# Two sigmoids behind the next unit's first copy, and a VectorE product behind the doubling, in the last batch of an attention and feed-forward kernel

## The chip, the cores and the metric

The kernel runs on one core of one Trainium2 chip. The metric is the device time of one launch in microseconds, the median of several runs. Five engines work side by side, each through its own queue in order: TensorE (PE) multiplies matrices into PSUM, ScalarE (ACT) applies functions, VectorE (DVE) and GpSimd (POOL) do elementwise work, and SyncE (SP) issues most transfers. An instruction that must wait for another engine holds all that stands behind it on its own queue.

## The reference

The first half is clustered attention: each query and key is assigned to the nearest of 16 centroids by cosine, and a query sees only the keys of its own cluster. The second half is a feed-forward layer with a sigmoid gate over the 3072 tokens (4 batches of 768) that the attention gives.

```python
mask = q_assign[:, :, :, None] == k_assign[:, :, None, :]
scores = np.where(mask, scale * np.matmul(q, k.transpose(0, 1, 3, 2)), -1e9)
attn = softmax(scores)                  # over the keys
x = (attn @ v).transpose(0, 2, 1, 3).reshape(B * S, H * D)     # 3072 x 512
gate = 1.0 / (1.0 + np.exp(-(x @ w_gate)))                     # 512 -> 1536
val = x @ w_val
return (gate * val @ w_out).astype(np.float32)                 # 1536 -> 512
```

Batch is 4, heads 8, sequence 768, head size 64.

## The kernel before

Attention goes batch by batch and head by head: scores (line 1064), an exponential on ScalarE (1069), the product with the values (1087). The feed-forward of one batch is worked off in small pieces between the attention steps of the next. The last batch has no next attention to hide behind, so its feed-forward stands at the end of the program in an order written out by hand, in `closing` (from line 651). This is the stage that the change touches; it begins near 271 us of the 318 us span.

`closing` computes gate and value for the last batch in tiles of 128 features by 384 tokens, and it saves multiplications: a 2 by 2 block (two feature tiles, two token halves) is made by Strassen's scheme in Winograd's form with seven products instead of eight. Such a block is a `Unit`. There are five gate units `G` and four value units `V`, for the feature tiles 6, 2, 4, 8 and 10 (`FS`); a value unit's gate unit is `v.g`. A product is two matmuls of 128 by 384 (line 699), summed into PSUM. The steps of a unit are named after the product that they run:

- `p1` writes into bank x, which is then copied out to the SBUF tile c1: by ScalarE for a gate unit (`copy`, line 705), by VectorE times two for a value unit (line 714, "the doubling").
- `p6`, `p7` and `p4` add to the same bank x. After `p6` ScalarE copies x to c12, after `p7` to c22. A later product may add to x only when the copy before it is done. After `p4` a gate unit's x goes through ScalarE's sigmoid to c21 (line 749), and a value unit's x is multiplied by VectorE with the gate's c21 into the hidden tile (line 745).
- `p5` writes bank y, `p3` adds to it; `p2` writes a bank z of its own. VectorE adds z to c1 (`p2`), y to c22 (`sum22`) and, after `p3`, y to c12 (lines 656 and 657).
- When c1, c22 and c12 of a gate unit are complete, `gate` puts ScalarE's sigmoid on each in place (line 758). When those of a value unit are complete, POOL multiplies them with the gate's (line 708).

Bank x of a gate unit is one of the two banks of `op`, bank x of a value unit one of the two of `avp`; y and z come from the four banks of `ring`. Gate and value units are interleaved with a lag: one turn of the loop at line 780, a "period" below, runs the gate unit g = G[n], the value unit v = V[n-1] before it, and the last product `p3` of the gate unit l = G[n-1] and of the value unit V[n-2]. There are four periods. Period 1 has 13 products, as V[n-2] does not exist yet; the others have 14. In periods 3 and 4 VectorE also starts on sums of hidden tiles for the output (`extra`). Behind the last period come `p3` of the last two units, the plain value products of G[4] (`u.v`), and the output products, which need 20.5 us to the end.

The queues take the instructions in the order in which `seq` lists the steps. On ScalarE a period before is: copy c1 of g, copy c12 of g, copy c12 of v, sigmoid of c12 of l, copy c22 of g, copy c22 of v, sigmoid into c21, sigmoid of c1, sigmoid of c22. On VectorE: doubling of v, sum into c12 of l, sum into c12 of V[n-2], the extra sums, sum into c1 of g, into c22 of g, into c22 of v, into c1 of v, and the product from v's bank x.

Of the kernel before, what the change touches and what calls it, by code (L numbers as in the profile page):

```python
# [11 lines left out]
ALU = mybir.AluOpType  # L12
# [88 lines left out]
def kernel(  # L101
# [12 lines left out]
    PE, ACT, DVE, POOL, SP = nc.tensor, nc.scalar, nc.vector, nc.gpsimd, nc.sync  # L114
# [53 lines left out]
    def out_bank():  # L168
        taken["op"] += 1
        return op.tile([128, DM], FP, tag="o", name="o")  # L170
# [326 lines left out]
    HB = {}  # L497
# [136 lines left out]
    def fin_plain(xT, fc, blk):  # L634
        b, st = B - 1, []

        def gate():
            if fc == 0:
                need(*(("x", b, p, 3 * blk + c) for p in range(NP) for c in range(3)))
                HB[b, blk] = htp.tile([128, NFC, 384], HP, name="hT")  # L640
            g = fin_group(xT, 0, fc, blk)
            st.append(thp.tile([128, 384], FP, name="th"))
            ACT.activation(st[0], g, AF.Sigmoid, scale=2.0)

        return [(NDC * 163, gate), (NDC * 163, lambda: hidden(xT, fc, blk, st[0]))]
# [5 lines left out]
    def closing(xT):  # L651
# [3 lines left out]
        b = B - 1  # L655
# [6 lines left out]
        for _ in range(8):  # L662
            t = tp.tile([128, 12, 128], HP, tag="T", name="T")
            v = t.rearrange("p c x -> p (c x)").bitcast(FP)
# [13 lines left out]
        class Unit:  # L678
# [31 lines left out]
            def p1(u):  # L710
                u.x = (avp.tile([128, 512], FP, tag="av", name="av") if u.w else out_bank())[:, 0:384]
                u.mm(u.x, 1, True, True)
                if u.w:
                    DVE.tensor_scalar(u.c1, u.x, 2.0, None, ALU.mult)
                else:
                    u.copy(u.c1)

            def p5(u, bk=None):
                u.y = (bk or bank(512, name="y"))[:, 0:384]
                u.mm(u.y, 5, True, True)  # L720
# [20 lines left out]

            def p4(u):
                u.mm(u.x, 4, False, True)
                if u.w:
                    DVE.scalar_tensor_tensor(
                        HB[b, 0][:, u.f], u.x, 2.0, u.g.c21, ALU.mult, ALU.mult
                    )
                else:
                    ACT.activation(u.c21, u.x, AF.Sigmoid, scale=2.0)

            def p3(u):
                u.mm(u.y, 3, False, True)
                (twice if u.w else plus)(u.c12, u.y, u.c12)
                if u.w:
                    u.gated(1, 1, u.c12, u.g.c12)
# [8 lines left out]
        def part(i, m, c0=0, c1=HF):  # L764
            return lambda: m.make(i, c0, c1)
# [3 lines left out]
        V = [Unit(1, n, f) for n, f in enumerate(FS[:-1])]  # L769
        for g, v in zip(G, V):  # L770
            v.g = g
        u = G[0]
        w = [f for fc in range(FC0) for _, f in fin_plain(xT, fc, 1)]
        seq += [
            u.p1, w[0], lambda u=u: u.p5(avp.tile([128, 512], FP, tag="av", name="av")), u.p6, w[1],
            u.p2, u.p7, lambda u=u: u.gate(u.c1), w[2], u.sum22, w[3], u.p4, lambda u=u: u.gate(u.c22),
        ]
        none = lambda: None
        extra = {3: [part(1, m0, 0, 2)], 4: [part(2, m0, 0, 2), part(3, m0)]}
        for n in range(1, len(G)):  # L780
            g, v, l = G[n], V[n - 1], G[n - 1]
            seq += [
                g.p1, v.p1, l.p3, V[n - 2].p3 if n > 1 else none,
                *extra.get(n, []), g.p6, g.p5, v.p6, lambda l=l: l.gate(l.c12), g.p2, g.p7, g.sum22, v.p5, v.p7, v.sum22,
                g.p4, v.p2, lambda g=g: g.gate(g.c1), v.p4, lambda g=g: g.gate(g.c22),
            ]

        def pair(m, bk):
# [49 lines left out]
        p0, l0 = pair(m0, lambda z: out_bank())  # L838
        pa, la = pair(ma, lambda z: avp.tile([128, 512], FP, tag="av", name="av"))
        pb, lb = pair(mb, lambda z: bank(512, name="o_end"))  # L840
        u = G[-1]
        seq += [
            u.p3, lambda: u.gate(u.c12), V[-1].p3, p0(1), lambda: u.v(0), lambda: u.v(1), pa(1),
            lambda: u.v(2), part(1, m0, 2), part(2, m0, 2), pb(1), lambda: u.v(3), l0([(0, HD)]),
            part(1, ma), part(2, ma), la([(0, HD)]), part(1, mb), p0(6), part(2, mb), p0(5),
            part(3, ma), part(4, m0), pa(6), pa(5), part(3, mb), p0(7), part(4, ma), pb(6),
# [655 lines left out]
    def halved(b):  # L1502
        return SCHED.get(f"halved{b}", 4 if b == 0 else 1)
# [9 lines left out]
    for b in range(B):  # L1513
        u = BASE[b]
# [77 lines left out]
    for p in range(NP):  # L1592
        plan(f"ql{p}", 0, lambda p=p: (done.add(f"ql{p}"), load_chunks(SP, "q", p, 1)))
        for i in range(1, NPT):
            u = RUSE[p, i]
# [3 lines left out]
    for p in range(NP):  # L1599
        u = USE[0, p, 0]  # L1600
# [87 lines left out]
    for b in range(1, B):  # L1688
        for p in range(NP):
            use = USE[b, p, 0]  # L1690
            o = SCHED.get(f"b1p{p}ld", -76) if b == 1 else SCHED.get("b2ld", -76)
# [8 lines left out]
    for b in range(B):  # L1700
        xT = xtp.tile([128, NDC, S], HP, tag="xTb", name="xTb")
        key = min(b, 1)
        for i in range(2 if b else NPT):
            u = BASE[b] + (DONE0[i] if b == 0 else 96 - 12 * halved(b) if i == 0 else 96)
# [30 lines left out]
    assert not bg, sorted(bg)  # L1735
    ffn_run(1e9)
    queue.extend(closing(xT))
    ffn_run(1e9)

# [29 lines left out]
```

## Time and profile before

| what | us |
|---|---|
| time, median of 3 runs | 320.72 (320.64 to 320.89) |
| profiled execution, its own time | 320.1 |
| its span | 318.3 |
| TensorE busy in the span | 310.5 |
| ScalarE, VectorE, POOL busy | 245.0, 238.6, 121.2 |
| period 1, 2, 3, 4 (start of g.p1 to the next) | 5.01, 4.78, 4.98, 4.78 |
| from the end of period 4 to the end of the span | 20.50 |

The profile is one execution, taken by the hardware profiler. In its rows "o" is bank x of a gate unit, "av" bank x of a value unit, "T" one of the tiles c1, c12, c22 and c21, and "hT" the hidden tile. A row such as "284.02 0.48 ACT L705 ..." has the start in us from the span's start, the length, the engine and the line; "[0.58 <-PE o L699]" says that the engine was idle 0.58 us before it and what ended that. Rows with x2 are two instructions taken together. The matmuls of one product overlap, so that a row of two is longer than the step to the next row.

### The profile page before, as it was taken

Reading aid. Unit: us, or ns where it says so; the run is one execution under the profiler, and the core shown is the slowest. Engines: PE = TensorE matmul, PEld = TensorE weight load, DVE = VectorE, ACT = ScalarE, POOL = GpSimd, SP = SyncE. Lnnn points to the kernel's source line nnn. Section 1 sums busy time; section 2 is a strip of 40 time slices with the busy share of each in tenths; the row PEclk is TensorE's granted clock in tenths of the full one; section 3 lists DMA queues with packets and bytes.
Section 4 is the critical chain, followed back from the end, with each engine's and each line's share of the span. In section 5 each row is a group of like instructions: output and inputs, shape, how many; then the busy total and the mean of one; then the engine's idle time right before and its main releaser. Section 6 shows DMA issues by size and latency. Waiting matters only on the chain.

```text
span 318.3 us, 9224 instructions
## 1 busy us (share of the span) xinstructions
PE 310.5 (98%) x3492; PEld 218.9 (69%) x3492; DVE 238.6 (75%) x623; ACT 245.0 (77%) x555; POOL 121.2 (38%) x157
## 2 busy tenths in 40 slices
PE   7899999999999999999999999999999999999995
PEld 5788666766766666666777678666777678655685
DVE  6899656777687677686778678776987777678883
ACT  6788988787889887877767786888877877588521
POOL 6887454144434275423133342524202111035600
PEclk9999999999999999999999999999999999999999
DMA  7999996748749988976775545882514131300014
GB/s 208 374 264 202 247 158 123 183 91 251 236 107 177 185 227 137 225 192 147 111 203 139 189 101 139 223 147 53 112 25 55 52 27 40 118 1 3 0 35 165
DMA packets 77996, 45.16 MB, mean 142 GB/s; under 512 B 56896, under 2 KB 75520, under 8 KB 77952
## 3 DMA queue, kind: packets, MB, share of 16 engines
q1 hardware_dynamic: 73840, 39.66, 51.7%
q0 software_dynamic: 3680, 4.72, 8.9%
q8 instruction: 27, 0.44, 0.6%
q10 hardware_dynamic: 432, 0.20, 0.2%
q14 instruction: 17, 0.14, 0.1%
HBM read 28.34 MB, written 6.29 MB: 109 GB/s over the span
## 4 chain that ended last, share of the span: by engine, by line
PE 88%; DMA 4%; DVE 3%; ACT 2%; SPq 1%; issue 1%; POOL 0%; ACTq 0%; DVEq 0%
PE sc L1064 18%; PE g L532 15%; PE v L548 15%; PE av L1087 10%; PE o L992 9%; PE o L863 5%; DMA qraw<-in_q_dram 4%; PE lg L436 2%; PE o_end L800 2%; PE o L699 2%; PE v L628 1%; ACT T L705 1%; PE av L699 1%; PE o L800 1%; PE av L800 1%; PE y L699 1%
## 5 line engine op out<-in xcount | busy, mean ns | idle before, releaser
L1069 ACT ACTIVATE es<-sc 128x384 f16<-128x384 f32 x384 | 174.1, 492 | 38.4 <-PE sc L1064 29.5
L1064 PE MATMUL sc<-T 128*128 128x384 f16 x384 | 117.3, 325 | 0.7 <-DVE T L1394 0.4
L1087 PEld LDWEIGHTS <-es 128*128 128x128 f16 x1152 | 81.3, 98 | 35.1 <-ACT es L1069 0.2
L1087 PE MATMUL av<-va,es 128*128 128x65 f16 x1152 | 97.6, 194 | 0.0
L553 DVE SCALAR_TENSOR_TENSOR hT<-th,v 128x384 f16<-128x384 f32 x72 | 39.8, 553 | 33.8 <-PE av L1087 29.6
L377 POOL TENSOR_TENSOR xp<-t,rec 128x384 f16<-128x384 f32 (+1 forms) x30 | 21.8, 726 | 97.3 <-DVE rec L374 49.2
L548 PE MATMUL v<-xTb,wv 128*128 128x384 f16 x288 | 58.5, 326 | 0.1
L532 PE MATMUL g<-xTb,wg 128*128 128x384 f16 x288 | 58.5, 326 | 0.0
L538 ACT ACTIVATE th<-g 128x384 f32<-128x384 f32 x72 | 35.4, 492 | 8.3 <-PE g L532 6.3
L1064 PEld LDWEIGHTS <-T 128*128 128x128 f16 x384 | 37.0, 96 | 1.2 <-DVE T L1394 0.7
L548 PEld LDWEIGHTS <-wv 128*128 128x128 f16 x288 | 28.0, 97 | 13.9 <-issue 0.3
L532 PEld LDWEIGHTS <-wg 128*128 128x128 f16 x288 | 27.9, 97 | 13.9
L1630 POOL TENSOR_TENSOR hl<-kraw,hl 128x384 f16<-128x384 f32 x22 | 20.2, 920 | 40.6 <-DVE hl L1629 23.4
L1630 POOL TENSOR_TENSOR hl<-qraw,hl 128x384 f16<-128x384 f32 x22 | 21.1, 961 | 11.1 <-DVE hl L1629 11.1
L863 PE MATMUL o<-wo,hT 128*128 128x512 f16 x72 | 19.9, 379 | 0.0
L372 DVE TENSOR_TENSOR t<-av,sv 128x390 f32<-128x390 f32 (+1 forms) x30 | 14.4, 480 | 7.0 <-PE av L1087 5.3
L708 POOL TENSOR_TENSOR hT<-T 128x384 f16<-128x384 f32 x12 | 12.2, 1037 | 16.8 <-DVE T L657 16.8
L939 DVE TENSOR_TENSOR ob<-o,ob 128x256 f32<-128x256 f32 (+1 forms) x28 | 15.0, 549 | 4.7 <-PE o L992 3.2
L992 PE MATMUL o<-wo,hT 128*128 128x256 f16 x108 | 16.8, 272 | 0.0
L992 PEld LDWEIGHTS <-sum 128*128 128x128 f16 x144 | 14.0, 97 | 3.3
L451 DVE TENSOR_REDUCE lgs<-lg 128x192 f32<-128x384 f32 x23 | 12.7, 551 | 3.0 <-PE lg L436 2.9
L324 POOL CAST va<-vraw 128x768 f16<-128x768 f32 x15 | 13.1, 874 | 1.8 <-DMA vraw<-in_v_dram 1.8
(225 smaller groups left out, 469.9 us busy)
## 6 DMA issues: line engine op xcount, KB each, us to landing
vraw<-in_v_dram SPq DMA_DIRECT2D x15, 384.0 KB, 5.1
kraw<-in_k_dram SPq DMA_DIRECT2D x14, 384.0 KB, 4.3
qraw<-in_q_dram SPq DMA_DIRECT2D x12, 384.0 KB, 4.2
out_dram<-ob SPq DMA_DIRECT2D x17, 256.0 KB, 2.2
wg<-in_moe_w_gate_dram POOLq DMA_DIRECT2D x2, 768.0 KB, 8.8
wv<-in_moe_w_val_dram POOLq DMA_DIRECT2D x2, 768.0 KB, 10.0
wo<-in_moe_w_out_dram POOLq DMA_DIRECT2D x2, 768.0 KB, 8.9
T<-ohT SPq DMA_DIRECT2D x44, 24.0 KB, 1.9
```

The source lines that it names most:

```text
L377: (eng or POOL).tensor_tensor(x, t[:, 0:nq, 0:64], bcast(rec[:, 0:nq], 64), ALU.mult)
L532: PE.matmul(out=g[:, 0:n], lhsT=wg[fc // WQ][:, dc, fc % WQ, :], rhs=xT[:, dc, t0 : t0 + n], start=(dc == 0), stop=(dc == NDC - 1),)
L538: ACT.activation(th[:, 0:n], g[:, 0:n], AF.Tanh)
L548: PE.matmul(out=w[:, 0:n], lhsT=wv[fc // WQ][:, dc, fc % WQ, :], rhs=xT[:, dc, t0 : t0 + n], start=(dc == 0), stop=(dc == NDC - 1),)
L553: DVE.scalar_tensor_tensor(HB[b, blk][:, fc, 0:n], st[0][:, 0:n], 1.0, w[:, 0:n], ALU.add, ALU.mult)
L863: PE.matmul(out=o, lhsT=HB[b, blk][:, fc, bass.ts(t, 128)], rhs=wo[fc // WON][:, fc % WON, :], start=(fc == 0), stop=(fc == NFC - 1),)
L939: plus = lambda dst, a, z: DVE.tensor_tensor(dst, a, z, ALU.add)
L992: PE.matmul(out=st[z][:, e], lhsT=a[:, c, :], rhs=rhs[:, c, :], start=start and c + e == 0, stop=c == HF - 1, skip_group_check=True,)
L1064: PE.matmul(out=sc.rearrange("p (c t) -> p c t", t=128), lhsT=s["k"], rhs=s["q"], start=True, stop=True,)
L1069: ACT.activation(es, sc, AF.Exp, scale=SCALE)
L1087: PE.matmul(out=av[:, a0 + s["c0"] + i, :], lhsT=s["es"][:, bass.ts(i, 128)], rhs=VA[b, p][:, e, s["j"], :], start=(first and i == 0 and a ...
L1630: POOL.tensor_tensor(hl[:, :, 64:128], r, hl[:, :, 0:64], ALU.subtract)
```

## The change

Three moves in `closing`, none of which adds or removes an instruction:

- The sigmoid of c22 of a gate unit goes from the end of its period to behind the next gate unit's copy of c1, and the sigmoid of c12 of that old unit follows it there, directly behind `l.p3`, ahead of the copies of c12 and c22.
- VectorE's doubling is taken out of `p1` and stands behind `l.p3`, so that the sum into c12 of l comes before it.
- VectorE's product from the value unit's bank x is taken out of `p4` and stands one period later, behind the doubling of the next value unit and behind the sum into c12 of its own unit (`o.p3`).

On ScalarE a period then is: copy c1 of g, sigmoid of c22 of l, sigmoid of c12 of l, copy c12 of g, copy c12 of v, copy c22 of g, copy c22 of v, sigmoid into c21, sigmoid of c1. On VectorE: sum into c12 of l, doubling of v, sum into c12 of V[n-2], product from the bank of V[n-2], the extra sums, and the four sums as before. TensorE's order of products, POOL's and the transfers' are unchanged.

```diff
             def p1(u):
                 u.x = (avp.tile([128, 512], FP, tag="av", name="av") if u.w else out_bank())[:, 0:384]
                 u.mm(u.x, 1, True, True)
-                if u.w:
-                    DVE.tensor_scalar(u.c1, u.x, 2.0, None, ALU.mult)
-                else:
+                if not u.w:
                     u.copy(u.c1)
+
+            def double(u):
+                DVE.tensor_scalar(u.c1, u.x, 2.0, None, ALU.mult)
...
             def p4(u):
                 u.mm(u.x, 4, False, True)
-                if u.w:
-                    DVE.scalar_tensor_tensor(
-                        HB[b, 0][:, u.f], u.x, 2.0, u.g.c21, ALU.mult, ALU.mult
-                    )
-                else:
+                if not u.w:
                     ACT.activation(u.c21, u.x, AF.Sigmoid, scale=2.0)
+
+            def out21(u):
+                DVE.scalar_tensor_tensor(HB[b, 0][:, u.f], u.x, 2.0, u.g.c21, ALU.mult, ALU.mult)
...
-            u.p2, u.p7, lambda u=u: u.gate(u.c1), w[2], u.sum22, w[3], u.p4, lambda u=u: u.gate(u.c22),
+            u.p2, u.p7, lambda u=u: u.gate(u.c1), w[2], u.sum22, w[3], u.p4,
...
             g, v, l = G[n], V[n - 1], G[n - 1]
+            o = V[n - 2] if n > 1 else None
             seq += [
-                g.p1, v.p1, l.p3, V[n - 2].p3 if n > 1 else none,
-                *extra.get(n, []), g.p6, g.p5, v.p6, lambda l=l: l.gate(l.c12), g.p2, g.p7, g.sum22, v.p5, v.p7, v.sum22,
-                g.p4, v.p2, lambda g=g: g.gate(g.c1), v.p4, lambda g=g: g.gate(g.c22),
+                g.p1, lambda l=l: l.gate(l.c22), v.p1, l.p3, lambda l=l: l.gate(l.c12),
+                v.double, *([o.p3, o.out21] if o else []), *extra.get(n, []),
+                g.p6, g.p5, v.p6, g.p2, g.p7, g.sum22, v.p5, v.p7, v.sum22, g.p4, v.p2,
+                lambda g=g: g.gate(g.c1), v.p4,
             ]
...
-            u.p3, lambda: u.gate(u.c12), V[-1].p3, p0(1), lambda: u.v(0), lambda: u.v(1), pa(1),
+            lambda: u.gate(u.c22), u.p3, lambda: u.gate(u.c12), V[-1].p3, V[-1].out21, p0(1), lambda: u.v(0), lambda: u.v(1), pa(1),
```

More of the change, by code (lines that the diff above doesn't have):

```diff
@@ L775, in closing @@
             u.p1, w[0], lambda u=u: u.p5(avp.tile([128, 512], FP, tag="av", name="av")), u.p6, w[1],
-            u.p2, u.p7, lambda u=u: u.gate(u.c1), w[2], u.sum22, w[3], u.p4, lambda u=u: u.gate(u.c22),
+            u.p2, u.p7, lambda u=u: u.gate(u.c1), w[2], u.sum22, w[3], u.p4,
         ]
-        none = lambda: None
         extra = {3: [part(1, m0, 0, 2)], 4: [part(2, m0, 0, 2), part(3, m0)]}
```

## The prediction

> **What bounds the kernel now.** I read the page first, then the windows of the closing stage, the chain that ended last, and the timeline of two periods.
>
> ```profile
> span 318.3 us, 9224 instructions
> PE 310.5 (98%) x3492; PEld 218.9 (69%) x3492; DVE 238.6 (75%) x623; ACT 245.0 (77%) x555; POOL 121.2 (38%) x157
> ...
> PE 88%; DMA 4%; DVE 3%; ACT 2%; SPq 1%; issue 1%; POOL 0%; ACTq 0%; DVEq 0%
> ```
>
> TensorE is busy for 98% of the span and carries 88% of the chain. A change on ScalarE and VectorE can move the end only through the few places where TensorE waits. The change lies in the four periods in which a gate unit g is paired with the value unit v before it. A window from one g.p1 to the next gives each period, and the last one what follows (the granted clock, PEclk, is 1.00 in all):
>
> ```profile
> core 0: us, PE busy (x) PEld busy (x) DVE busy (x) ACT busy (x) POOL busy (x), PEclk, DMA share, GB/s
> 278.25:283.26 5.01, 4.55 (x28) 2.53 (x26) 3.12 (x7) 3.99 (x10) 0.00 (x0) 1.00 0.01 2
> 283.26:288.04 4.78, 4.71 (x30) 2.73 (x28) 3.95 (x10) 3.96 (x11) 2.96 (x3) 1.00 0.02 3
> 288.04:293.02 4.98, 4.71 (x31) 2.73 (x29) 4.16 (x11) 3.96 (x11) 2.96 (x3) 1.00 0.01 2
> 293.02:297.80 4.78, 4.71 (x30) 2.73 (x29) 4.54 (x12) 3.96 (x11) 3.35 (x3) 1.00 0.00 0
> 297.80:318.30 20.50, 17.18 (x153) 14.35 (x151) 13.11 (x30) 5.87 (x16) 2.94 (x3) 1.00 0.22 78
> ```
>
> Period 2 in the timeline, with start, length, engine and line in each row:
>
> ```profile
> 283.20 0.93 ACT L758 ACTIVATE T<-T 128x384 f32<-128x384 f32 x2
> 283.26 0.49 PE L699 MATMUL o<-xTb,wg 128*128 128x384 f16 x2
> 283.72 0.55 DVE L745 SCALAR_TENSOR_TENSOR hT<-av,T 128x384 f16<-128x384 f32 x1
> 283.91 0.49 PE L699 MATMUL y<-qraw,wg 128*128 128x384 f16 x2
> 284.02 0.48 ACT L705 ACTIVATE T<-o 128x384 f32<-128x384 f32 x1
> 284.18 0.55 DVE L714 TENSOR_SCALAR T<-av 128x384 f32<-128x384 f32 x1
> 284.56 0.49 PE L699 MATMUL o<-kraw 128*128 128x384 f16 x2
> 284.65 0.55 DVE L656 TENSOR_TENSOR T<-y,T 128x384 f32<-128x384 f32 x1
> 285.08 0.49 ACT L705 ACTIVATE T<-o 128x384 f32<-128x384 f32 x1 [0.58 <-PE o L699]
> 285.11 0.55 DVE L657 SCALAR_TENSOR_TENSOR T<-y,T 128x384 f32<-128x384 f32 x1
> 285.21 0.49 PE L699 MATMUL av<-kraw,hl 128*128 128x384 f16 x2
> 285.86 0.49 PE L699 MATMUL o<-qraw,kraw 128*128 128x384 f16 x2
> 286.12 0.52 ACT L758 ACTIVATE T<-T 128x384 f32<-128x384 f32 x1
> 286.54 0.48 ACT L705 ACTIVATE T<-o 128x384 f32<-128x384 f32 x1
> 287.07 0.48 PE L699 MATMUL o<-xTb,kraw 128*128 128x384 f16 x2
> 287.59 0.49 ACT L749 ACTIVATE T<-o 128x384 f32<-128x384 f32 x1
> ```
>
> A product is two matmuls; from g.p1 (283.26) to g.p7 (285.86) there are eight, so one takes 0.325 us, and it ends 0.49 after its start. Periods 2 to 4 hold 14 products, 4.55 us, so TensorE waits 0.23, 0.43 and 0.23 us in them; period 1 holds 13, 4.225 us, and waits 0.785. Together 1.675 us, which is also the most that this stage can give back. The place is seen at 287.07: g.p4 could have begun at 286.84, and waits for the copy of c22 (286.54), which ScalarE began only after the old unit's sigmoid (286.12, L758). Period 1 has a second wait:
>
> ```profile
> 278.24 0.56 DVE L649 SCALAR_TENSOR_TENSOR hT<-v,th 128x384 f16<-128x384 f32 x1 [0.33 <-ACT th L643]
> 278.25 0.49 PE L699 MATMUL o<-xTb,wg 128*128 128x384 f16 x2
> 278.45 0.49 ACT L749 ACTIVATE T<-o 128x384 f32<-128x384 f32 x1 [0.24 <-PE o L699]
> 278.58 0.49 PE L699 MATMUL av<-xTb,wv 128*128 128x384 f16 x2
> 278.84 0.51 ACT L758 ACTIVATE T<-T 128x384 f32<-128x384 f32 x1
> 278.90 0.49 PE L699 MATMUL av<-qraw,wg 128*128 128x384 f16 x2
> 279.10 0.56 DVE L714 TENSOR_SCALAR T<-av 128x384 f32<-128x384 f32 x1 [0.30 <-PE av L699]
> 279.25 0.48 ACT L705 ACTIVATE T<-o 128x384 f32<-128x384 f32 x1
> 279.79 0.48 PE L699 MATMUL o<-kraw 128*128 128x384 f16 x2 [0.39 <-ACT T L705]
> ```
>
> g.p6 (279.79) waits for the copy of c1 (279.25), which stood behind the sigmoid of c22 (278.84): 0.56 us late against 279.23.
>
> Some further rows of the timeline, from later places, for the prices below:
>
> ```profile
> 288.19 1.00 POOL L708 TENSOR_TENSOR hT<-T 128x384 f16<-128x384 f32 x1 [1.39 <-DVE T L657]
> ...
> 289.34 0.49 PE L699 MATMUL o<-kraw,qraw 128*128 128x384 f16 x2
> 289.93 0.49 ACT L705 ACTIVATE T<-o 128x384 f32<-128x384 f32 x1 [0.64 <-PE o L699]
> 290.31 0.49 PE L699 MATMUL z<-xTb,wg 128*128 128x384 f16 x2
> 290.91 0.56 DVE L656 TENSOR_TENSOR T<-z,T 128x384 f32<-128x384 f32 x1 [0.26 <-PE z L699]
> ...
> 300.02 1.21 DVE L649 SCALAR_TENSOR_TENSOR hT<-v,T 128x384 f16<-128x384 f32 x2 [0.29 <-PE v L628]
> ```
>
> **Prices.** ScalarE: the start after a copy or after L749 is 0.39 later (278.45 to 278.84), after a sigmoid L758 0.41 (two from 283.20 to 284.02); a copy is done after 0.49. VectorE: start to start 0.465 (283.72, 284.18, 284.65, 285.11), done after 0.55. From a product's end to its reader 0.03 (279.07 to 279.10; 285.05 to 285.08). From a copy's end to the matmul that it frees 0.05 (287.02 to 287.07). A copy that must also wait for POOL starts 0.10 after the product (289.34 + 0.49 to 289.93). No row of this stage shows a matmul that waits for VectorE. I take ScalarE's 0.05, the same kind of release; the bounds are 0 and the 0.11 with which VectorE itself follows a product in the row at 290.91, and over four periods they move the sum by -0.2 and +0.24.
>
> **The change, part by part.** No instruction is added or removed: the same 14 products, ScalarE's nine and VectorE's eight stay in each period, in another order. DMAs and the queues of SP and POOL keep theirs. Times below are from the start of g.p1 in a period of 14 products.
>
> *Sigmoid of c22 behind the next c1 copy.* The copy of c1 may start when g.p1 ends, 0.49 + 0.03 to 0.10, and is done by 1.08 at the latest; g.p6's place is 1.30, so TensorE does not wait. In periods 2 to 4 that copy already made it (284.02 + 0.48 against 284.56), so this gains nothing there. In period 1 the copy starts 0.39 after L749, at 278.84, is done at 279.32, and g.p6 starts at 279.37: 0.14 late instead of 0.56.
>
> *Sigmoid of c12 ahead of the copies.* It needs VectorE's sum into c12 (L656 after l.p3). With l.p3 at 0.65 to 1.14 that sum, now first, runs 1.17 to 1.72; the sigmoid starts at 1.76 (0.04 after) and the copy of c12 behind it at 2.17, done at 2.66. So g.p7 may start at 2.71; undisturbed its place is 2.60.
>
> *Doubling of v.p1 behind that sum.* Before, it came first: 284.18 is 0.92, done at 1.47, and v.p6, which adds to the same bank, had its place at 1.95. Now it is 1.17 + 0.465 = 1.635, done at 2.19, and v.p6 starts at 2.24: a new wait of 0.29. What is queued behind v.p6 on TensorE is everything: g.p2, g.p7 (2.24 + 0.65 = 2.89), v.p5, v.p7 (3.54), g.p4. It covers the wait for the copy of c12 (2.71).
>
> *Copy of c22 without the sigmoid before it.* g.p7 ends at 3.38; the copy, which waits for POOL too, starts at 3.48 and is done at 3.97; g.p4 starts at 4.02 against its place 2.89 + 0.975 = 3.865: a wait of 0.155 instead of 0.23. The copy for v.p4 (v.p7 ends 4.03, done 4.55) is in time for 4.67.
>
> *Product from the bank (L745) behind the doubling of the next period.* Its bank is one of two, and the next owner is v.p1 one period later still, so TensorE does not meet it. It takes one 0.465 place ahead of the sum into g.c1, which can start at about 3.05 instead of 2.86; that feeds only the sigmoid of c1, which stands behind L749, 0.52 after g.p4's start (287.07 to 287.59), so at 4.54 or later. In periods 3 and 4 the small sums for the output stand behind it (VectorE's busy time is 4.16 and 4.54 there against 3.95, so 0.2 and 0.6 us); they fill the time up to the copy of c22 (3.97), for which the next sum waits anyway. After the last p3 three VectorE instructions, as before, stand ahead of L649, which begins 2.2 after it (297.80 to 300.02) with 0.29 us idle before; they are done by 2.0. POOL's product for c12 starts about 0.25 later, and POOL idles 1.39 us after it (288.19). These count as nothing; if a cover went, its place would cost 0.465 us once.
>
> **Sum.** Periods 2, 3, 4: 0.29 + 0.155 = 0.445 each against 0.23, 0.43, 0.23, so +0.215, +0.015, +0.215. Period 1: 0.14 at g.p6; the sum at 279.42, the doubling 279.885 to 280.44, v.p6 at 280.49 against 280.02, 0.47; g.p4 0.155; together 0.765 against 0.785, so -0.02. In all +0.425 us. The profiled execution took 320.1 us (318.3 of span and 1.8 around it), so 320.5 for it; the median of the runs is 320.72, 0.6 above it, and I add the difference to the median: 321.14, given as 321.1 us.
>
> A rule against the change: the Trainium skill ("VectorE: DVE Perf Modes", The DRAIN you can't avoid) lets the next VectorE instruction start only when the pipe of the one before is empty. The rows above show 0.465 between starts of 0.55 long instructions, so here they overlap, and I go by the rows.
>
> **Rivals.** A fifth of a per cent, 0.64 us, is about what a measurement of this kernel can tell from no change.
>
> *v.p6 is not held* (the doubling is early enough or the bank frees sooner). For it: VectorE has idle time before the sum. Against: VectorE works in order and the sum cannot precede 1.17. Then the sigmoid of c12 takes its place: g.p7 waits until 2.71 (0.11), g.p4 0.155, 0.265 per period against 0.89 in three, and period 1 has 0.14 + 0.29 + 0.155 = 0.585. Together -0.3 us, 320.4: within the fifth. Chance 0.20.
>
> *Faster: neither holds TensorE.* If in addition the sum into c12 ended before about 1.6, the copy of c12 would make g.p7's place too: 4 x 0.155 + 0.14 = 0.76 against 1.675, -0.915 us, 319.8. It passes the mark when 0.64 of the 1.675 us go. The trace offers nothing that moves l.p3's end. Chance 0.09, with all that I overlook on this side.
>
> *Slower: the sum starts late.* L656 at 290.91 came 0.11 after its product, not 0.03. If the sum into c12 does so, the doubling and v.p6 come 0.08 later in all four periods: +0.32, in all +0.745, 321.5. It decides from 0.055 a period on. Against it: that row waits for two engines, the moved one for TensorE alone. A pause as in period 3 (0.43 instead of 0.23 at the same place) would do the same. Chance 0.33.
>
> *VectorE starts only when the instruction before has ended*: the doubling comes 0.55, not 0.465, after the sum, 0.085 four times, 321.5. The rows of period 2 speak against it. This is what the DRAIN section of the Trainium skill, named above, would make of it. Chance 0.03.
>
> **How the numbers follow.** My forecast has 0.35. Faster 0.09; slower 0.33 + 0.03 = 0.36, and 0.04 from the upper end of the forecast's own spread (0.1 us for each of four periods), so 0.40; same 0.51. The range reaches from the first rival to just above the third, 320.3 to 321.8; the likeliest case alone spans 320.8 to 321.5.
>
> **What would show it.** Right: TensorE waits at v.p6 (L699, av) for VectorE's doubling in all four periods, about 0.3 us, 0.5 in the first; g.p4's wait falls to about 0.15; g.p6 of period 1 starts near 279.4; the periods measure about 4.99, 4.99, 5.00, 5.00 us. Wrong: v.p6 follows g.p5 after 0.325, or a period shorter than 4.78, or any change of the time after the last p3 (20.50 us before, to the end of the span).

## The result and the profile after

The changed kernel took 321.63 us (median of 12 runs, 321.26 to 322.93) against 320.83 us (12 runs, 320.35 to 321.61) for the kernel before on the same chips: ratio 1.003, 95% interval 1.0017 to 1.0044, so 0.5 to 1.4 us slower. The forecast was 321.1 us, the range 320.3 to 321.8.

The page of the changed kernel, and its windows from one g.p1 to the next (lines behind 711 have moved by a few: 717 is the doubling, 749 the product from the bank, 746 the sigmoid into c21, 908 to 912 the sums for the output). In the experiments some are off by one or two again:

```profile
span 320.4 us, 9224 instructions
PE 312.5 (98%) x3492; PEld 220.4 (69%) x3492; DVE 240.2 (75%) x623; ACT 245.9 (77%) x555; POOL 121.0 (38%) x157
```

```profile
279.43:284.37 4.94, 4.62 (x29) 2.52 (x26) 3.02 (x6) 4.03 (x10) 0.00 (x0) 1.00 0.01 2
284.37:289.36 4.99, 4.85 (x29) 2.72 (x28) 4.14 (x9) 4.16 (x11) 2.97 (x3) 1.00 0.01 3
289.36:294.35 4.99, 4.85 (x30) 2.72 (x28) 4.44 (x10) 4.16 (x11) 2.96 (x3) 1.00 0.01 2
294.35:299.76 5.41, 5.03 (x31) 2.73 (x29) 5.06 (x11) 4.58 (x12) 2.96 (x3) 1.00 0.00 0
299.76:320.40 20.64, 17.32 (x152) 14.35 (x151) 13.44 (x30) 5.52 (x15) 2.92 (x3) 0.99 0.22 77
```

The first number behind the window is its length. The change did not touch what comes before 279 us; this execution lost 1.18 us there, and it was itself one of the longer ones (322.2 us), so the span is no measure of the change. From g.p1 of period 1 to the end of the span it is 40.97 us against 40.05 before, 0.92 us more, which agrees with the ratio (0.96 us).

| stretch | before | after | difference | forecast |
|---|---|---|---|---|
| period 1 | 5.01 | 4.94 | -0.07 | -0.02 |
| period 2 | 4.78 | 4.99 | +0.21 | +0.215 |
| period 3 | 4.98 | 4.99 | +0.01 | +0.015 |
| period 4 | 4.78 | 5.41 | +0.63 | +0.215 |
| from the last u.p3 on | 20.50 | 20.64 | +0.14 | 0 |

Period 2 of the changed kernel in the timeline:

```profile
285.02 0.49 PE L699 MATMUL y<-qraw,wg 128*128 128x384 f16 x2
285.54 0.56 DVE L656 TENSOR_TENSOR T<-y,T 128x384 f32<-128x384 f32 x1 [0.49 <-PE y L699]
285.99 0.49 PE L699 MATMUL y<-kraw 128*128 128x384 f16 x2
286.02 0.55 DVE L717 TENSOR_SCALAR T<-av 128x384 f32<-128x384 f32 x1
286.13 0.52 ACT L758 ACTIVATE T<-T 128x384 f32<-128x384 f32 x1 [0.34 <-DVE T L656]
286.62 0.49 PE L699 MATMUL av<-kraw,hl 128*128 128x384 f16 x2
287.26 0.49 PE L699 MATMUL o<-qraw,kraw 128*128 128x384 f16 x2
287.85 0.49 ACT L705 ACTIVATE T<-o 128x384 f32<-128x384 f32 x1 [0.22 <-PE o L699]
288.39 0.48 PE L699 MATMUL o<-xTb,kraw 128*128 128x384 f16 x2
```

The sum into c12 (285.54) follows l.p3 by 0.03, the doubling (286.02) comes behind it and ends at 286.57, and v.p6 starts at 286.62 where 286.315 was its place: 0.305 us of waiting. g.p4 (288.39) is 0.155 behind its place. Both waits are those of the forecast, to 0.015 us. Period 4 has a wait that was not forecast:

```profile
296.93 0.55 DVE L749 SCALAR_TENSOR_TENSOR hT<-av,T 128x384 f16<-128x384 f32 x1
297.16 1.00 POOL L708 TENSOR_TENSOR hT<-T 128x384 f16<-128x384 f32 x1 [0.41 <-ACT T L705]
297.40 0.91 DVE L910 TENSOR_TENSOR sum<-sum,hT 128x256 f16<-128x256 f16 x1
297.83 0.49 ACT L705 ACTIVATE T<-o 128x384 f32<-128x384 f32 x1 [0.22 <-PE o L699]
298.23 0.55 DVE L912 TENSOR_TENSOR sum<-hT 128x768 f16<-128x768 f16 x1
298.70 0.54 DVE L656 TENSOR_TENSOR T<-z,T 128x384 f32<-128x384 f32 x1
299.16 0.54 DVE L656 TENSOR_TENSOR T<-y,T 128x384 f32<-128x384 f32 x1
299.63 0.54 DVE L657 SCALAR_TENSOR_TENSOR T<-y,T 128x384 f32<-128x384 f32 x1
299.76 0.48 PE L699 MATMUL y<-qraw,wg 128*128 128x384 f16 x2 [0.25 <-DVE T L656]
300.22 0.48 PE L699 MATMUL y<-qraw,wv 128*128 128x384 f16 x2
```

The sums for the output are one small sum (128x256) in each of periods 3 and 4, and behind that of period 4 a long one (128x768). Both small sums last 0.91 us in the changed kernel; in period 3 too, where it makes no wait:

```profile
292.40 0.91 DVE L908 TENSOR_TENSOR sum<-hT 128x256 f16<-128x256 f16 x1
```

In the kernel before, the small sums lasted 0.28, and in period 4 POOL's product, beside the long sum, was the one that was stretched:

```profile
290.37 0.28 DVE L907 TENSOR_TENSOR sum<-hT 128x256 f16<-128x256 f16 x1
...
295.34 0.28 DVE L909 TENSOR_TENSOR sum<-sum,hT 128x256 f16<-128x256 f16 x1
295.54 0.55 DVE L911 TENSOR_TENSOR sum<-hT 128x768 f16<-128x768 f16 x1
295.57 1.38 POOL L708 TENSOR_TENSOR hT<-T 128x384 f16<-128x384 f32 x1 [0.48 <-DVE T L657]
```

So VectorE reaches the sum into c22 (299.16) only 0.84 us after the copy that it needs was done (297.83 + 0.49). It ends at 299.70; the last u.p3, which adds to the same bank y, starts at 299.76 instead of 299.35 (0.41 late), and V.p3 at 300.22 behind the next sum (299.63), another 0.135 behind its own place.

### The profile page after: what moved, and what is told of

Read it like the earlier page. It is cut to its first block, busy times and chain, and to the rows that moved or that the text cites. A ratio compares the mean times of both kernels' runs of the same rounds, so it can differ in the third digit from the quotient of the medians.

```text
span 320.4 us, 9224 instructions
## 1 busy us (share of the span) xinstructions
PE 312.5 (98%) x3492; PEld 220.4 (69%) x3492; DVE 240.2 (75%) x623; ACT 245.9 (77%) x555; POOL 121.0 (38%) x157
```

## The experiments

My theory after the result: three things decide. (1) v.p6 waits for the doubling; (2) the sum into c12 gates both the doubling and the sigmoid of c12, so putting either in front makes the other late; (3) the small sums, pushed behind the product from the bank, run into POOL's product and make the sum into c22 late in period 4. The rivals stand with each run. All times are medians, beside runs of the kernel before on the same chip (320.76 us for the small sums earlier, the doubling in front, the sigmoid of c22 alone and both sigmoids; 320.71 us for the others). The ratio, with its 95% interval, is an estimate of its own and can differ by 0.1% from the quotient of the two medians. The intervals reach 0.4 to 0.8 us to either side, so I read the mechanism from the periods of the one profiled execution.

**The small sums earlier.** From the changed kernel:

```diff
-                v.double, *([o.p3, o.out21] if o else []), *extra.get(n, []),
-                g.p6, g.p5, v.p6, g.p2, g.p7, g.sum22, v.p5, v.p7, v.sum22, g.p4, v.p2,
+                v.double, *([o.p3, o.out21] if o else []),
+                g.p6, g.p5, v.p6, g.p2, *extra.get(n, []), g.p7, g.sum22, v.p5, v.p7, v.sum22, g.p4, v.p2,
```

> The changed kernel with the small sums of periods 3 and 4 (extra) moved from behind the product from the bank to behind VectorE's sum into c1 of g (after g.p2). Theory (the sums were stretched from 0.28 to 0.91 us because POOL's product runs at the time, and they ended only 0.14 after it; that made the sum into c22 late, and the last u.p3 and V.p3 waited 0.40 and 0.13 for it): in period 3 the sum starts near 3.5 after g.p1 and still ends 0.14 after POOL's product, so lasts about 0.44; in period 4 the first lasts about 0.43; the sum into c22 of period 4 comes 0.4 earlier than in the changed kernel, u.p3 has no wait, period 4 measures 4.99 instead of 5.41. About 0.5 us less than the changed kernel: 0.3 to 0.4 us above the kernel before. Rival (the sum is long because it follows a write of the same tile by VectorE itself): it becomes 0.28 long wherever another instruction stands between. Rival (u.p3 is held by something else): period 4 stays at 5.41.

Measured: 321.14 us, ratio 1.0015 (0.9998 to 1.0033). Periods 4.94, 4.99, 5.00 and 4.99; V.p3 is still 0.095 late, which I had not expected. VectorE and POOL in period 4 of this run, and the window:

```profile
296.89 1.00 POOL L708 TENSOR_TENSOR hT<-T 128x384 f16<-128x384 f32 x1 [0.60 <-ACT T L705]
297.25 0.56 DVE L656 TENSOR_TENSOR T<-z,T 128x384 f32<-128x384 f32 x1
297.72 0.31 DVE L910 TENSOR_TENSOR sum<-sum,hT 128x256 f16<-128x256 f16 x1
297.96 0.54 DVE L912 TENSOR_TENSOR sum<-hT 128x768 f16<-128x768 f16 x1
298.43 0.54 DVE L656 TENSOR_TENSOR T<-y,T 128x384 f32<-128x384 f32 x1
```

```profile
294.08:299.07 4.99, 4.85 (x29) 2.73 (x28) 4.40 (x11) 4.16 (x11) 2.96 (x3) 1.00 0.00 0
```

The sum into c22 starts at 298.43, 4.35 after g.p1 instead of 4.81, and u.p3's wait is gone: 5.41 has become 4.99, as (3) says. The sum ends at 298.03, 0.14 after POOL's product (297.89), as in the changed kernel (298.31 and 298.16). But it started later than I expected and so lasted 0.31, too near to 0.28 to tell POOL from the rival with the write of the same tile. That took the next run.

**POOL's product later.** In period 3 of the changed kernel only, POOL's product for c12 is issued behind that for c22; VectorE's order and every wait on its own writes stay.

```diff
-            def p3(u):
+            def p3(u, late=False):
...
-                if u.w:
+                if u.w and not late:
                     u.gated(1, 1, u.c12, u.g.c12)
...
-                v.double, *([o.p3, o.out21] if o else []), *extra.get(n, []),
-                g.p6, g.p5, v.p6, g.p2, g.p7, g.sum22, v.p5, v.p7, v.sum22, g.p4, v.p2,
+                v.double, *([lambda o=o, n=n: o.p3(n == 3), o.out21] if o else []), *extra.get(n, []),
+                g.p6, g.p5, v.p6, g.p2, g.p7, g.sum22, v.p5, v.p7, v.sum22,
+                *([lambda o=o: o.gated(1, 1, o.c12, o.g.c12)] if n == 3 else []), g.p4, v.p2,
```

> The changed kernel with POOL's product for c12 of period 3 alone issued one place later on POOL, behind that for c22; so POOL is idle when VectorE's small sum of period 3 runs, and as before in period 4 up to its new place. Theory (VectorE's half precision sum is held while POOL works on the same memory): the sum of period 3 lasts 0.28 instead of 0.91, in the same place behind the same product. Rival (it lasts long because it follows a write of the same tile by VectorE): 0.91 again. The time is that of the changed kernel or a little off; the length of this one instruction is the question.

Measured: 321.46 us, ratio 1.0017 (0.9994 to 1.004). The rows of VectorE and POOL:

```profile
291.41 0.55 DVE L749 SCALAR_TENSOR_TENSOR hT<-av,T 128x384 f16<-128x384 f32 x1
291.88 0.28 DVE L909 TENSOR_TENSOR sum<-hT 128x256 f16<-128x256 f16 x1
...
294.07 3.94 POOL L708 TENSOR_TENSOR hT<-T 128x384 f16<-128x384 f32 x4 [3.03 <-DVE T L657]
...
296.87 0.28 DVE L911 TENSOR_TENSOR sum<-sum,hT 128x256 f16<-128x256 f16 x1
297.07 1.36 DVE L913 TENSOR_TENSOR sum<-hT 128x768 f16<-128x768 f16 x1
```

With POOL idle the sum of period 3 (291.88) lasts 0.28, in the same place behind the same product; the rival falls. In period 4 POOL now runs four products without a break to 298.01: the long sum (297.07) cannot run beside the last of them and lasts 1.36 instead of 0.55. It ends at 298.43, 0.42 after POOL. The small sum of period 4 (296.87) began when the third of the four had 0.11 us left, kept its 0.28 us, and the fourth product, from 296.95, lasted 1.06 instead of 1.00. With the long sum later, u.p3 waits 0.585 and period 4 measures 5.58.

**The doubling in front again.** From the changed kernel:

```diff
-                g.p1, lambda l=l: l.gate(l.c22), v.p1, l.p3, lambda l=l: l.gate(l.c12),
-                v.double, *([o.p3, o.out21] if o else []), *extra.get(n, []),
+                g.p1, lambda l=l: l.gate(l.c22), v.p1, v.double, l.p3, lambda l=l: l.gate(l.c12),
+                *([o.p3, o.out21] if o else []), *extra.get(n, []),
```

> The changed kernel with the doubling put back in front of the sum into c12. Theory (the sum into c12 is what both the doubling and the sigmoid of c12 hang on): the wait of 0.29 at v.p6 goes, but the sum starts at 1.32 instead of 1.17, the sigmoid of c12 and the copy of c12 come 0.15 later, and g.p7 waits until 2.86 against its place 2.60, 0.26 us; g.p4 keeps 0.155. Periods 1 to 3: 4.97, 4.97, 4.97, so 0.03 less each at most; period 4 stays above 5.2. The time stays 0.6 to 0.9 us above the kernel before. Rival (only the doubling's place cost time): periods of 4.70, about 1 us less than the changed kernel, faster than before.

Measured: 321.14 us, ratio 1.0014 (0.9996 to 1.0031). Periods 4.90, 4.96, 5.02 and 5.16. TensorE's waits have moved, as (2) says:

```profile
280.39 0.49 PE L699 MATMUL av<-kraw,hl 128*128 128x384 f16 x2
...
281.48 0.48 PE L699 MATMUL o<-qraw,kraw 128*128 128x384 f16 x2 [0.28 <-ACT T L705]
```

These are v.p6, now in its place, and g.p7 of period 1, 0.44 us late (281.48 against 280.39 + 0.65) behind the copy of c12. In period 2 g.p7 is 0.265 late (286.38 against 285.79 + 0.325), in period 3 0.335. The rival's 4.70 is far off: 0.03 to 0.04 us in periods 1 and 2, and nothing in period 3, is all that the doubling's place is worth as long as the sigmoid of c12 stands ahead of the copies. Two figures of the expectation were missed. The medians differ by 0.4 us from the kernel before, not by 0.6 to 0.9, and period 4 fell to 5.16, not above 5.2: the small sum starts 2.79 after g.p1 (296.29) instead of 3.05, lasts 0.91 again, and the sum into c22 is 0.25 earlier, so that u.p3 waits only 0.125.

**The product from the bank alone.** From the kernel before:

```diff
-                    DVE.scalar_tensor_tensor(
-                        HB[b, 0][:, u.f], u.x, 2.0, u.g.c21, ALU.mult, ALU.mult
-                    )
...
-                g.p1, v.p1, l.p3, V[n - 2].p3 if n > 1 else none,
+                g.p1, v.p1, l.p3, *([V[n - 2].p3, V[n - 2].out21] if n > 1 else []),
...
-            u.p3, lambda: u.gate(u.c12), V[-1].p3, p0(1), lambda: u.v(0), lambda: u.v(1), pa(1),
+            u.p3, lambda: u.gate(u.c12), V[-1].p3, V[-1].out21, p0(1), lambda: u.v(0), lambda: u.v(1), pa(1),
```

> The kernel before with only VectorE's product from the value unit's bank moved behind the next period's sums into c12 (and ahead of the extra sums); ScalarE and the doubling as before. Theory: periods 1 to 3 as before (5.01, 4.78, 4.78 to 4.98), since the product's place is free there. In periods 3 and 4 the small sums now meet POOL's product and last 0.85 to 0.91 us instead of 0.28; in period 4 the sum into c22 comes late, u.p3 waits about 0.3 and V.p3 about 0.1: 0.4 us above before. Rival (the product hides everywhere, as the prediction had it): no change.

Measured: 320.94 us, ratio 1.0002 (0.9978 to 1.0026), which decides nothing by itself. The periods are 5.01, 4.78, 4.78 and 5.15. Both small sums last 0.91 and end 0.15 after POOL's product; u.p3 waits 0.37 and V.p3 0.145:

```profile
295.59 1.00 POOL L708 TENSOR_TENSOR hT<-T 128x384 f16<-128x384 f32 x1 [0.19 <-DVE T L657]
295.83 0.91 DVE L908 TENSOR_TENSOR sum<-sum,hT 128x256 f16<-128x256 f16 x1
```

So the waits of u.p3 and V.p3 come with this part of the change alone. Period 3 lost the 0.2 us by which it was longer than its neighbours before; more on that below.

**The sigmoid of c12 alone.** From the kernel before:

```diff
-                g.p1, v.p1, l.p3, V[n - 2].p3 if n > 1 else none,
-                *extra.get(n, []), g.p6, g.p5, v.p6, lambda l=l: l.gate(l.c12), g.p2, g.p7, g.sum22, v.p5, v.p7, v.sum22,
+                g.p1, v.p1, l.p3, lambda l=l: l.gate(l.c12), V[n - 2].p3 if n > 1 else none,
+                *extra.get(n, []), g.p6, g.p5, v.p6, g.p2, g.p7, g.sum22, v.p5, v.p7, v.sum22,
```

> The kernel before with only the sigmoid of c12 moved ahead of the copies, directly behind l.p3; the sigmoid of c22 and VectorE as before. Theory: with the doubling first the sum into c12 is done at 1.94, the sigmoid starts at 1.98, the copy of c12 is done at 2.88 and g.p7 waits until 2.93 against its place 2.60 (0.33), g.p4 0.155: period 2 and 4 5.03, period 3 5.03, period 1 4.96. About 0.5 us above before. Rival (taking the sigmoid from between the copies is a gain wherever it goes): periods 2 and 4 of 4.70, 0.2 us below before.

Measured: 321.47 us, ratio 1.0013 (0.999 to 1.0035). Periods 4.90, 5.15, 5.39 and 5.03; 20.47 us together against 19.55, 0.92 more, while the medians differ by 0.76. g.p7 is 0.03 late in period 1 and 0.47, 0.395 and 0.325 in the others, and period 3 has a pause besides (g.p4 0.445 late instead of 0.155; more on that below):

```profile
286.36 0.48 PE L699 MATMUL o<-qraw,kraw 128*128 128x384 f16 x2 [0.30 <-ACT T L705]
...
291.45 0.49 PE L699 MATMUL o<-qraw 128*128 128x384 f16 x2 [0.24 <-ACT T L705]
...
292.87 0.48 PE L699 MATMUL o<-xTb,qraw 128*128 128x384 f16 x2 [0.28 <-ACT T L705]
...
296.77 0.49 PE L699 MATMUL o<-qraw 128*128 128x384 f16 x2 [0.17 <-ACT T L705]
```

The cost is above the expected 0.5 us: besides the pause, the doubling of period 2 starts 1.06 after g.p1 (284.36), where I had the 0.92 of the kernel before, and the sum into c12 behind it is as much later. This part of the change costs by the place to which the sigmoid goes, not by leaving the old one.

**The sigmoid of c22 alone.** From the kernel before:

```diff
-            u.p2, u.p7, lambda u=u: u.gate(u.c1), w[2], u.sum22, w[3], u.p4, lambda u=u: u.gate(u.c22),
+            u.p2, u.p7, lambda u=u: u.gate(u.c1), w[2], u.sum22, w[3], u.p4,
...
-                g.p1, v.p1, l.p3, V[n - 2].p3 if n > 1 else none,
+                g.p1, lambda l=l: l.gate(l.c22), v.p1, l.p3, V[n - 2].p3 if n > 1 else none,
...
-                g.p4, v.p2, lambda g=g: g.gate(g.c1), v.p4, lambda g=g: g.gate(g.c22),
+                g.p4, v.p2, lambda g=g: g.gate(g.c1), v.p4,
...
-            u.p3, lambda: u.gate(u.c12), V[-1].p3, p0(1), lambda: u.v(0), lambda: u.v(1), pa(1),
+            lambda: u.gate(u.c22), u.p3, lambda: u.gate(u.c12), V[-1].p3, p0(1), lambda: u.v(0), lambda: u.v(1), pa(1),
```

> The kernel before with only the sigmoid of c22 moved behind the next c1 copy. Theory: period 1 loses the wait at g.p6 (0.56 to 0.14) and measures about 4.60; periods 2 to 4 stay at 4.78, 4.98 or 4.78, 4.78, since there the copy of c1 was in time anyway. About 0.4 us less than before, 0.13%. Rival (the move costs in the other periods what it gains in the first): no change.

Measured: 320.10 us, ratio 0.9978 (0.9961 to 0.9995): 0.13% faster was expected, and the interval just excludes no change. Periods 4.60, 4.78, 4.98 and 4.78; only the first has changed, by 0.41.

**Both sigmoids, that of c12 only one place forward.** The edit above, and

```diff
-                *extra.get(n, []), g.p6, g.p5, v.p6, lambda l=l: l.gate(l.c12), g.p2, g.p7, g.sum22, v.p5, v.p7, v.sum22,
+                *extra.get(n, []), g.p6, lambda l=l: l.gate(l.c12), g.p5, v.p6, g.p2, g.p7, g.sum22, v.p5, v.p7, v.sum22,
```

> The kernel before with the sigmoid of c22 moved as in the change, and the sigmoid of c12 moved only one place forward, behind the copy of c12 and ahead of the copy of c12 of the value unit; VectorE as before. Theory: the sum into c12 (1.32 to 1.87) is done when ScalarE gets to the sigmoid (2.2), the copy of c22 starts 0.10 after g.p7, and only g.p4 waits, 0.155 a period: periods of 4.52, 4.71, 4.71, 4.71, about 0.9 us less than before (0.28% faster). Rival (ScalarE's sigmoid delays the copy of c12 of v and so v.p7 by as much): no change against the run with c22 alone.

Measured: 320.01 us, ratio 0.9974 (0.9961 to 0.9988). Periods 4.46, 4.70, 4.99 and 4.70. Three of them are the theory's to 0.06; the third kept its pause, and this takes 0.28 of the 0.9 us that I expected; together they are 0.70 us shorter than before. The run with c22 alone was 0.41 shorter, so the rival, no change against it, fails in the periods by 0.29 us; the medians (320.10 and 320.01) do not tell the two runs apart.

**And v.p2 ahead of g.p4.** The last edit with, on TensorE,

```diff
-                g.p4, v.p2, lambda g=g: g.gate(g.c1), v.p4,
+                v.p2, g.p4, lambda g=g: g.gate(g.c1), v.p4,
```

> The version with the sigmoid of c22 moved and that of c12 behind the copy of c12, and v.p2 put ahead of g.p4 on TensorE, so that the copy of c22 has one product more to hide behind. Theory: g.p4 no longer waits, v.p4 waits about 0.085 for the copy of c22 of v; periods 4.45, 4.64, 4.64 (up to 4.9 if the pause before the copy of c22 in period 3 is there again), 4.64; 1.0 to 1.2 us below before, 0.3 us below the version without the swap. Rival (the wait only changes its place, to v.p4): as without the swap.

Measured: 319.07 us against 320.71 us, ratio 0.9942 (0.9918 to 0.9966). TensorE no longer waits at g.p4, but for 0.105 us in period 3, and v.p4 waits 0.055 to 0.095. The windows:

```profile
279.78:284.24 4.46, 4.46 (x29) 2.53 (x26) 3.02 (x6) 3.76 (x9) 0.00 (x0) 1.00 0.01 2
284.24:288.88 4.64, 4.64 (x30) 2.73 (x29) 4.00 (x9) 3.96 (x10) 2.97 (x3) 1.00 0.02 4
288.88:293.59 4.71, 4.71 (x30) 2.72 (x29) 4.02 (x10) 3.82 (x10) 2.96 (x3) 1.00 0.01 2
293.59:298.22 4.63, 4.63 (x29) 2.73 (x28) 4.60 (x11) 3.98 (x10) 3.35 (x3) 1.00 0.00 0
```

18.44 us against 19.55, 1.11 us less, which is the expectation; the medians differ by 1.64, and their interval (1.1 to 2.6 us) just holds it. The periods are 0.41 us shorter than without the swap, 0.28 of it in period 3, so the rival falls. Against the kernel before, this is the only version that is faster by half a per cent.

## Why the prediction was right, and which term was too small

The measured time lies in the range, and the direction of the sum is right; the size is 0.92 us by the profile against 0.425. The likeliest case, a change within a fifth of a per cent, did not come: the ratio of 1.003 lies beyond that mark, the slower case to which I gave 0.40, with an interval that begins just inside it. That the range held was in part luck: 321.63 us lies above the span of the likeliest case (320.8 to 321.5), in the part that was there for a rival that did not happen.

*The bound.* Right that TensorE's waits in this stage are the whole matter. But 0.14 us of the 0.92 lies behind the last u.p3, in V.p3's wait, and u.p3's own 0.41 makes period 4 5.41 instead of 5.00. Both belong to the term that failed below, and any change of the 20.50 us was on the prediction's list of what would show it wrong.

*Sigmoid of c22.* Right, and shown alone: it frees g.p6 of period 1 (0.145 late, forecast 0.14) and nothing else; -0.41 us.

*Sigmoid of c12 and doubling.* Right: v.p6 waits 0.295 to 0.305 (forecast 0.29), in period 1 0.475 (0.47), and g.p4 0.145 to 0.155 (0.155) in periods 2 to 4. In period 1 g.p4 waits 0.085 where I had 0.155: I gave the copy of c22 the 0.10 of a wait for two engines, and it started 0.03 after g.p7. This is why period 1 did 0.05 better.

*Product from the bank.* Here the prediction failed. The step was "In periods 3 and 4 the small sums ... fill the time up to the copy of c22 (3.97), for which the next sum waits anyway", with 0.2 and 0.6 us for the sums. I took the lengths from a kernel in which they start before POOL's product. One place later the small sum of each period starts beside it and lasts until it has ended, 0.63 us longer. In period 3 the cover was still enough. In period 4, with the second sum behind the first, it was not: the sum into c22 came at 4.81 after g.p1, and u.p3 and V.p3 waited 0.41 and 0.135. The price that I named for a lost cover, 0.465 us, was near, but I gave it no chance. The row that shows the mechanism stood in the profile of before: POOL's product at 295.57, 1.38 long instead of 1.00, next to the sum at 295.54. A page bears on it too. The Trainium skill ("SBUF — State Buffer", SBUF: two separate sides, with its part Who interferes with whom) says that a VectorE instruction with two SBUF inputs contends with a GpSimd instruction that reads SBUF, and that whichever comes first blocks the other fully. The rows agree, in both orders: 0.91 and 1.36 us for the sums behind POOL, 1.38 for POOL behind a sum. All but 0.13 us of a sum's own length comes after POOL's end (0.15 of 0.28, 0.42 of 0.55).

*The rivals.* "v.p6 is not held" and "neither holds TensorE" are out: v.p6 is held in all four periods. In the run with the doubling in front, v.p6 was free, and the sigmoid of c12 took its place at g.p7, where the first rival put the next wait; it was 0.26, not 0.11, because the sum into c12 then stands behind the doubling. "The sum starts late" is out as a cause, though the time that it gave, 321.5 us, is near the measured one: the sum into c12 starts 0.03 after l.p3. "VectorE starts only when the instruction before has ended", is out for these forms: 285.54 to 286.02 is 0.48 between starts of 0.56 long instructions. So the sentence of the Trainium skill ("VectorE: DVE Perf Modes", The DRAIN you can't avoid) on which this rival rested does not describe this pair; the same paragraph ends by saying that a next instruction that is not held starts earlier, and that agrees.

*Open.* In the kernel before, period 3 is 0.2 us longer than its neighbours, because the copy of c22 (291.50) starts 0.2 us later than its sigmoid (290.90 + 0.41) and its product (290.64 + 0.49) explain:

```profile
290.64 0.49 PE L699 MATMUL o<-qraw 128*128 128x384 f16 x2
...
290.90 0.52 ACT L758 ACTIVATE T<-T 128x384 f32<-128x384 f32 x1
...
291.50 0.49 ACT L705 ACTIVATE T<-o 128x384 f32<-128x384 f32 x1
```

In the run with both sigmoids, that of c12 one place forward, the same copy shows a pause for which the trace finds no releaser ("issue"):

```profile
291.71 0.49 ACT L705 ACTIVATE T<-o 128x384 f32<-128x384 f32 x1 [0.31 <-issue]
```

The pause is there in the five kernels that leave the product from the bank in its place and gone in the five that move it; in the latter the trace shows a semaphore instruction of its own ahead of the sigmoid into c21, three times, and in the others none. None of the runs tells what makes the pause. So the forecast of period 3 (+0.015) came true in part by luck: it let these 0.2 us go with the sigmoid, and they went with the product.

## What to carry to other kernels

When an instruction is moved, take the length of each neighbour that it pushes from a place where the same engines run beside it; here a half precision VectorE sum of two SBUF operands (128x256) took 0.28 us with POOL idle and 0.91 us when it started 0.24 us into a POOL product. When several steps hang on one sum (here the doubling, the sigmoid and two copies), bringing one of them forward only moves the wait; look for the place at which the inputs are long there, which here was one position forward (0.29 us less in the periods than with the sigmoid of c22 alone), while the front, with the doubling ahead of it, cost 0.92 us. A wait at the end of a chain (copy of c22 to g.p4) can be hidden by giving TensorE one more independent product in between, which took 0.41 us off the periods here.

## What the runs showed of the hardware that I had not expected

A half precision VectorE sum of two SBUF tiles does not run beside POOL's product: the small sum ended 0.14 to 0.15 us after the POOL instruction in eight places (in periods 3 and 4 of the changed kernel, of the runs with the sums earlier and the doubling in front, and of the run with the product alone; for example 298.31 after 298.16, and 298.03 after 297.89), whether it started 0.23 or 0.84 us after POOL. VectorE instructions that read PSUM and one SBUF tile kept their 0.54 to 0.56 us beside POOL (297.25 beside 296.89, with the sums earlier). Where the sum came first, at 295.54, it kept its 0.55 us and POOL's product became 0.38 us longer.
